# First loads on a second queue, early weight fetches and plain last stores in a fused attention, MoE and FFN kernel

## The chip, the cores and the metric
The kernel runs on one core of a Trainium2 chip. The metric is device time in microseconds (us) of one execution, lower is better. TensorE multiplies matrices (PE in the profile, PEld its weight loads); VectorE (DVE), ScalarE (ACT) and GpSimd (POOL) work on elements; SyncE (SP) issues most DMAs. A q behind an engine's name (SPq, POOLq) marks its sequencer.

## The reference
The output (2304 x 512, f32) is made in three parts:
```
scores = scale * q @ k^T            # q, k, v: (4, 8, 576, 64)
scores = where(block_i >= block_j, scores, -1e9)   # blocks of 64
x = (softmax(scores) @ v)           # tokens 2304 x 512
e = argmax(x @ w_gate)              # 8 experts, one per token
x = gate[e] * (relu(x @ w1[e]) @ w2[e])            # 512 -> 1024 -> 512
out = softplus(x @ w_in) @ w_out    # 512 -> 2048 -> 512
```

## The kernel before
**Precision.** Every f32 operand is split into a high and a low part (`h`, `l`), and each product is three matmuls: high by high, low by high, high by low. ScalarE casts the high part, VectorE subtracts it for the low one.

**Stages.** Attention runs over 16 pairs of heads (4 batches of 8 heads): k and q are transposed on TensorE (`prep_pe`, L315 to L326, K and Q in the order below; `a` for the first 512 rows, `b` for the last 64), split into `kZ` and `qZ`, and scores, exponentials, transposes and products follow. Batch 0 is loaded by `load_first` (L267 to L274) head by head, in calls f0, f1 and on; the other batches by `load_raw` (b1.0 and on). Between them the constants are set (p0 to p36, `mrow` among them) and, with `et`, the routing's tables. Then 12 slots of 256 tokens of one expert each go through the MoE: gather (g), transposes (X), first layer (A), second layer (C), output copy on ScalarE (yo, L981) and scatter by GpSimd into `yd` (sc, L986), with the weights loaded (d) and split (h1, l1, h2, l2) per slot. Slots that only other inputs need lie behind a nest of branches (`more`, L1430 to L1436). The FFN takes the tokens in groups of 4, 4, 4, 4 and 2 tiles of 128: it loads `yg` (fl for group 0, y1 to y4 after it), transposes it (fx0t to fx3t, x1.0.t and on), runs the first layer over 16 column blocks f with weights `HB[f]` (P, L1119 to L1121: 12 matmuls per group and f) and softplus (a), and stores the result to DRAM (`gd`). The second layer takes 8 chunks per group: a chunk's two blocks are loaded (N g.c.0, tile `gq`, three buffers in turn), sums of quarters are made and split (N g.c.1 to N g.c.5, `ah` and `al`), and seven products are added up instead of eight (Q, 42 matmuls a chunk in the groups of four tiles, banks X, Y, Z and M). o combines the banks into `fos`, O writes 128 rows to the output.

**Second-layer weights.** The sums of w_out's quarters are made and split during the first layer (w, s). Those of chunks 0 to 3 stay in SBUF; those of 4 to 7 are stored to `wd` in DRAM and come back by `fetch` (W4 to W7, two tiles of 896 KB each) into the pool that `second_pools` (e2, L1445) opens when the first layer's tiles are closed. A fetch waits for the last use of what lay there.

**Output rows.** The MoE's scatter puts the tokens into `yd` in a new order, and each row carries its token number in a last column; `OI` keeps it, and `done` (L1301 to L1307) scatters each finished tile to those rows by an indirect DMA of GpSimd.

**What sets the order.** One string, `SCHEDULE` (line 46), names every call; the loop at L1450 runs them one after the other, and each call appends its instructions to its engines' queues. So an engine works through its own instructions in the string's order, and one that waits holds up all behind it on that engine:
```python
        for key in SCHEDULE.split():
            if key in calls:
                calls.pop(key)()
```
Of the kernel before, what the change touches and what calls it, by code (L numbers as in the profile page):

```python
# [112 lines left out]
l17+1 lr39 h27+1 lr43 l20+1 yo1+0 lr44 l21+1 sc1+0 lr45 l22+1 lr46 A0+1 lr47 lg1 d10+2 lr49 lg2 lr50 lg3 lg4 g0+2 l23+1  # L113
d11+2 lg5 l24+1 g1+2 d12+2 lg6 l25+1 A1+1 lg7 d13+2 hh0+1 l26+1 lg8 lg9 lg10 hl0+1 lg11 d20+2 lg12 lg14 l27+1 h10+2
d21+2 l10+2 A2+1 d22+2 hh1+1 h12+2 hl1+1 d23+2 l12+2 lg15 h14+2 h16+2 l14+2 A3+1 hh2+1 l16+2 hl2+1 h11+2 lg16 h13+2
l11+2 X0+2 h15+2 l13+2 C0+1 d10+3 hh3+1 l15+2 xh0+2 d11+3 hl3+1 h17+2 C1+1 h20+2 xl0+2 d12+3 lg17 l17+2 h21+2 X1+2
l20+2 d13+3 C2+1 xh1+2 l21+2 xl1+2 d20+3 h22+2 C3+1 g0+3 l22+2 h23+2 C4+1 g1+3 l23+2 lg13 h24+2 d21+3 C5+1 l24+2 h25+2
C6+1 l25+2 h26+2 d22+3 C7+1 l26+2 yo0+1 sc0+1 A0+2 h27+2 yo1+1 l27+2 sc1+1 d23+3 A1+2 hh0+2 hl0+2 h10+3 h12+3 l10+3
A2+2 h14+3 l12+3 hh1+2 l14+3 h16+3 hl1+2 l16+3 A3+2 hh2+2 hl2+2 h11+3 h13+3 l11+3 X0+3 h15+3 l13+3 C0+2 d10+4 hh3+2
l15+3 xh0+3 d11+4 hl3+2 h17+3 C1+2 h20+3 xl0+3 d12+4 l17+3 h21+3 X1+3 l20+3 d13+4 C2+2 g0+4 xh1+3 l21+3 xl1+3 d20+4  # L120
g1+4 h22+3 C3+2 l22+3 h23+3 C4+2 l23+3 h24+3 d21+4 lg18 l24+3 C5+2 lg19 lg20 lg21 more v0+0 v1+0 v0+1 v1+1 h25+3 C6+2
# [604 lines left out]
def late_routing(nc, K, L, m, rows_of, big, wide, B):  # L726
# [763 lines left out]
```

## Time and profile before
| | |
|---|---|
| median of 3 runs | 939.73 us (937.86 to 939.75) |
| the profiled execution | 940.5 us, of which the span is 938.8 |
| mean granted clock | 0.993 |
| VectorE, ScalarE, GpSimd busy | 71%, 60%, 16% |
| DMA | 149.17 MB, mean 159 GB/s |

The span runs from the first to the last instruction; 1.7 us of the time lie around it. Busy shares are means over stages with different limits, so a change in one stage is read from the rows of that stage. The page's 40 slices of 23.5 us show TensorE at nine tenths or more but in the first, in the slices about 730 to 800 (8 and 9) and in the last (4):
```profile
PE   6999999999999999999999999999999989999994
```

### The profile page before, as it was taken

The numbers are of one execution on the slowest core, as the hardware profiler recorded it, in microseconds if no ns is written. First come the engines' busy times: TensorE is split into PE (matmuls) and PEld (weight loads), VectorE is DVE, ScalarE is ACT, GpSimd is POOL, SyncE is SP. The second block draws the span as 40 slices with busy tenths as digits, with TensorE's granted clock in tenths as the row PEclk, the third lists the DMA queues.
The fourth block names the chain that finished last, engine by engine and source line by source line (L and its number), as shares of the span: only waits on it lengthen the run. The fifth ranks groups of instructions, "written<-read, shape, count | busy, mean of one in ns | idle before, by whom it ended". The sixth has DMA issues, their size and how long they took to land.

```text
span 938.8 us, 18304 instructions
## 1 busy us (share of the span) xinstructions
PE 901.2 (96%) x6331; PEld 796.9 (85%) x6331; DVE 664.0 (71%) x1471; ACT 566.9 (60%) x1256; POOL 146.0 (16%) x183
## 2 busy tenths in 40 slices
PE   6999999999999999999999999999999989999994
PEld 4888888777999889999999887888789988999994
DVE  3766778885997888666664367686675479798874
ACT  3677676685755657555553487887788533334331
POOL 2000000010163142222221000000000003131512
PEclk9999999999999999999999999999999999999997
DMA  5984644213526398766520366556655673434421
GB/s 125 194 159 81 139 83 132 87 50 116 170 65 224 113 300 265 239 220 210 177 86 23 118 213 220 175 190 235 235 206 198 229 288 128 142 113 136 133 80 59
DMA packets 134645, 149.17 MB, mean 159 GB/s; under 512 B 70543, under 2 KB 92047, under 8 KB 134544
## 3 DMA queue, kind: packets, MB, share of 16 engines
q1 hardware_dynamic: 129264, 132.17, 46.5%
q0 software_dynamic: 5280, 15.75, 4.9%
q8 instruction: 51, 0.84, 0.4%
q14 instruction: 50, 0.41, 0.2%
HBM read 120.09 MB, written 41.96 MB: 173 GB/s over the span
## 4 chain that ended last, share of the span: by engine, by line
PE 54%; DVE 6%; DMA 3%; ACT 2%; issue 1%; SPq 0%; POOLq 0%; DVEq 0%; ACTq 0%
PE yps L975 3%; PE yps L977 3%; PE yps L976 3%; PE fh L1120 3%; PE hps L955 3%; PE fh L1119 3%; PE fh L1121 3%; PE hps L956 3%; PE hps L957 3%; DMA gq<-gd 2%; PE fX L1120 2%; PE fX L1121 2%; PE fX L1119 2%; PE fY L1120 2%; PE fY L1121 2%; PE fz L1275 2%
## 5 line engine op out<-in xcount | busy, mean ns | idle before, releaser
L1242 ACT CAST ah<-sum 128x1280 fp32r<-128x1280 f32 (+1 forms) x40 | 46.2, 1156 | 113.9 <-issue 46.0
L955 PE MATMUL hps<-xh,H1h 128*128 128x256 f32 x384 | 109.2, 284 | 1.5 <-ACT y L981 1.5
L956 PE MATMUL hps<-xl,H1h 128*128 128x256 f32 x384 | 108.7, 283 | 0.3 <-DVE xl L945 0.3
L957 PE MATMUL hps<-xh,H1l 128*128 128x256 f32 x384 | 108.6, 283 | 0.0
L383 ACT ACTIVATE P<-s,negm 128x448 f32<-128x448 f32 (+4 forms) x160 | 82.7, 528 | 25.5 <-DVE negm L378 25.5
L918 DVE TENSOR_TENSOR H2l<-R,H2h 128x512 fp32r<-128x512 f32 x96 | 67.2, 716 | 26.8 <-ACT H2h L914 26.8
L378 DVE TENSOR_REDUCE negm<-s 128x1 f32<-128x576 f32 (+4 forms) x160 | 68.2, 479 | 20.5 <-PE s L372 20.5
L975 PE MATMUL yps<-H2h,hh 128*128 128x512 f32 x192 | 77.2, 402 | 1.9 <-PEq L1432 1.9
L1303 POOL DMA_INDIRECT out_dram<-fos,OI x18 | 45.2, 2512 | 214.0 <-DVE fos L1299 177.2
L914 ACT CAST H2h<-R 128x512 fp32r<-128x512 f32 x96 | 58.0, 621 | 31.9 <-DVE H2l L918 17.8
L955 PEld LDWEIGHTS hps<-xh,H1h 128*128 128x128 f32 x384 | 73.5, 192 | 2.5 <-ACT y L981 1.7
L977 PE MATMUL yps<-H2l,hh 128*128 128x512 f32 x192 | 74.9, 390 | 0.0
L976 PE MATMUL yps<-H2h,hl 128*128 128x512 f32 x192 | 74.8, 389 | 0.0
L956 PEld LDWEIGHTS hps<-xl,H1h 128*128 128x128 f32 x384 | 73.6, 192 | 0.9 <-DVE xl L945 0.5
L918 DVE TENSOR_TENSOR H1l<-R,H1h 128x512 fp32r<-128x512 f32 x96 | 64.1, 706 | 13.4 <-ACT H1h L914 12.3
L957 PEld LDWEIGHTS hps<-xh,H1l 128*128 128x128 f32 x384 | 73.6, 192 | 0.0
L389 PE MATMUL pt<-ident,P 128*128 128x128 f32 x480 | 69.4, 282 | 2.7 <-DVE PT L394 2.0
L372 PE MATMUL s<-kZ,qZ 64*128 64x288 f32 (+4 forms) x576 | 64.2, 336 | 3.7 <-DVE qZ L343 1.5
L1246 DVE TENSOR_TENSOR al<-sum,ah 128x1280 fp32r<-128x1280 f32 (+1 forms) x40 | 54.1, 1352 | 19.1 <-ACT ah L1242 19.1
L914 ACT CAST H1h<-R 128x512 fp32r<-128x512 f32 x96 | 55.1, 619 | 18.8 <-PE hps L956 17.4
L372 PEld LDWEIGHTS s<-kZ,qZ 64*128 64x128 f32 x576 | 54.3, 198 | 12.1 <-issue 6.2
L1275 PE MATMUL fz<-Wh,al 128*128 128x256 f32 x216 | 61.8, 286 | 0.0
(287 smaller groups left out, 2608.5 us busy)
## 6 DMA issues: line engine op xcount, KB each, us to landing
R<-in_moe_w_dram SPq DMA_DIRECT2D x96, 512.0 KB
gd<-ft SPq DMA_DIRECT2D x64, 256.0 KB
gq<-gd SPq DMA_DIRECT2D x64, 256.0 KB
dbw<-in_moe_w_out_dram SPq DMA_DIRECT2D x32, 256.0 KB
dbl<-in_moe_w_in_dram SPq DMA_DIRECT2D x22, 256.0 KB
yg<-yd SPq DMA_DIRECT2D x4, 1026.0 KB
xd<-xs SPq DMA_DIRECT2D x16, 256.0 KB
wd<-ah SPq DMA_DIRECT2D x4, 896.0 KB
```

The costliest lines, as they stand in the source:

```text
L372: mm(o, lhsT=a, rhs=b, start=first, stop=last)
L383: nc.scalar.activation(t[0:n, 0:NK[c]], SC.pop((p, j, c))[0:n], AF.Exp, bias=NM.pop((p, j, c))[0:n], scale=1.0, accum_out=rs[p % 4][0:n, c ...
L389: nc.tensor.transpose(ps[:, o:o + 128], P[p, j, c][:, 128 * kc:128 * kc + 128], ident)
L914: nc.scalar.copy(HW[l, i][0], raw(l, i))
L918: TT(l_, raw(l, i), h.bitcast(F32), op=ALU.subtract)
L955: mm(a, lhsT=wh, rhs=xh, start=(k == 0), stop=False)
L956: mm(a, lhsT=wh, rhs=xl, start=False, stop=False)
L957: mm(a, lhsT=wl, rhs=xh, start=False, stop=(k == 3))
L975: mm(o, lhsT=h[:, c], rhs=wh, start=(f == 0), stop=False)
L976: mm(o, lhsT=l[:, c], rhs=wh, start=False, stop=False)
L977: mm(o, lhsT=h[:, c], rhs=wl, start=False, stop=(f == 7))
L1275: mm(o, lhsT=l, rhs=wh, start=False, stop=False)
```

## The change
- q's loads of heads 0 and 1 (four DMAs) are issued by ScalarE, first of all, with the table load `at` between them; SP's other first loads follow k directly, and v's of heads 0 and 1 come behind k and q of heads 2 and 3. `u0` adds seven bf16 matmuls of 512 columns on `mrow` before the first transposes, `u1` two more before the first scores. `et` moves behind the first pair's m01.
- The late routing places the tokens of the last two tiles (rows 2048 to 2303) in their own rows of `yd`, by five more VectorE operations; `done` writes these two tiles with two plain DMAs from SP in the place of two scatters.
- The empty case of each `tc.If` is laid out first.
- v0+5 and v1+5 (w_in's conversion) move behind yo1+3; fl moves behind sc1+10 and fx0t to fx3t behind C3+11, between C4+11 and C7+11; s5.5 to s5.7 move behind x3.3.
- `fetch` is called per tile. `e3` sets the tiles' places: the first three (W4.0, W4.1, W5.0) lie over HB[3], HB[5] and HB[7] and are fetched by GpSimd, which also issues chunk 2's load. SP fetches W5.1 behind N0.4.0, W6 behind N0.6.0, W7 behind N0.7.0.
- In the last group Q4.5.4 to Q4.5.6 move behind o4.0.2.

Of the string, pieces without the calls between them (`-` before, `+` now):
```diff
-p0 f0 f1 p1 f2 p2 f3 f4 p3 f5 p4 f6 p5 f7 f8 f9 f10 f11 f12 f13 p6
+f4 f5 at f6 f7 p0 f0 f1 p1 f2 p2 f3 p3 p4 p5 f8 f9 f10 f11 f12 f13 p6
...
-l26+4 v0+5 v1+5 A0+4 yo0+3 sc0+3 v2+5 yo1+3 v3+5
...
-a4.15.4 e2 N0.1.4 N0.2.0 W4 N0.1.5
+a4.15.4 e2 e3 W4.0 W4.1 W5.0 N0.1.4 N0.2.0 N0.1.5
```
Of the code:
```diff
-    def load_first(nm, h0, nh):
+    def load_first(nm, h0, nh, eng=nc.sync):
...
-        return [lambda o=o, i=i: nc.sync.dma_start(o, i) for o, i in l]
+        return [lambda o=o, i=i: eng.dma_start(o, i) for o, i in l]
...
+    calls["at"] = lambda: nc.scalar.preload_act_table_set("natural_log_exp_and_others")
+
+    def warm(n):
+        o = pso.tile([128, 512], F32, tag="o", name="warm")
+        for _ in range(n):
+            mm(o.rearrange("p (a b) -> p a b", a=4), lhsT=mrow, rhs=mrow.unsqueeze(1).to_broadcast([128, 4, 128]), start=True, stop=True)
+
+    calls.update(u0=lambda: warm(7), u1=lambda: warm(2))
-    first = load_first("k", 0, 2) + load_first("q", 0, 2) + load_first("v", 0, 2) + load_first("k", 2, 2) + load_first("q", 2, 2) + gates + load_first("v", 2, 2)
+    first = load_first("k", 0, 2) + load_first("q", 0, 2, nc.scalar) + load_first("k", 2, 2) + load_first("q", 2, 2) + load_first("v", 0, 2) + gates + load_first("v", 2, 2)
...
+        lambda: TT(xs, C[:, :, T - 1:T], Gx[:, :, T - 2:T - 1], op=ALU.subtract),
+        lambda: V.tensor_tensor_scan(xc, xs.rearrange("p e o -> p (e o)"), K["z"][:, 0:G], 0.0, op0=ALU.add, op1=ALU.add),
+        lambda: TT(xs, xc.unsqueeze(2), xs, op=ALU.subtract),
+        lambda: TT(Z, Z, bc(xs, 128, G, T), op=ALU.subtract),
...
+        lambda: TT(dm[:, T - 2:T], tk[:, T - 2:T, 0], tk[:, T - 2:T, 1], op=ALU.add),
...
-    def fetch(c):
-        W[c] = [P["wrest"].tile([128, 7 * QW], F32R, tag=f"W{x}{c}", name=f"W{x}{c}", bufs=1) for x in "hl"]
-        for j in range(2):
-            nc.sync.dma_start(W[c][j].bitcast(F32), wd[c, j])
+    def rest():
+        for c, j in ((5, 1), (6, 0), (6, 1), (7, 0), (7, 1), (4, 0), (4, 1), (5, 0)):
+            W.setdefault(c, [None, None])[j] = P["wrest"].tile([128, 7 * QW], F32R, name=f"W{'hl'[j]}{c}")
+
+    def fetch(c, j):
+        (nc.gpsimd if (c, j) in ((4, 0), (4, 1), (5, 0)) else nc.sync).dma_start(W[c][j].bitcast(F32), wd[c, j])
...
-                nc.sync.dma_start(t[:, j, 0:w], gd[16 * g + c + 8 * j, :, 0:w])
+                (nc.gpsimd if n == 2 else nc.sync).dma_start(t[:, j, 0:w], gd[16 * g + c + 8 * j, :, 0:w])
...
+        if i >= NT // 128 - 2:
+
+            nc.sync.dma_start(out[128 * i:128 * i + 128], st["out", g, u][:, 2 * j:2 * j + 2].rearrange("p a b -> p (a b)"))
+            return
...
-                    nest.enter_context(tc.If(n > s - EARLY))
+                    nest.enter_context(tc.If(n > s - EARLY, preferred_fallthrough_block=False))
```
ScalarE's queue at the start, before and now (`psT` is the bank of the transposes; a number behind a tile's name is only its buffer):
```order
L1371 ACT_TABLE_LOAD
L338 ACTIVATE kZ<-psT 128x512
L338 ACTIVATE qZ<-psT 128x512
L338 ACTIVATE qZ<-psT_259 128x64
L338 ACTIVATE kZ<-psT_259 128x64
```
```order
L274 DMA qraw<-in_q_dram 128x4x64 x2
L486 ACT_TABLE_LOAD
L274 DMA qraw<-in_q_dram 64x2x64 x2
L338 ACTIVATE kZ<-psT 128x512
L338 ACTIVATE qZ<-psT 128x512
```
Four DMAs of q stand ahead of ScalarE's first casts, two on either side of the table load.

SP's queue behind the last stores of the first layer (L1137, now L1153), before and now (L1213, now L1231, is a fetch of a weight tile; L1223, now L1241, a chunk's load):
```order
L1137 DMA gd<-ft 128x256 x16
L1223 DMA gq_12916<-gd 128x512 x2
L1213 DMA Wh_12919<-wd 128x1792
L1213 DMA Wl_12920<-wd 128x1792
L1223 DMA gq_12936<-gd 128x512 x2
L1213 DMA Wh_12939<-wd 128x1792
L1213 DMA Wl_12940<-wd 128x1792
L1223 DMA gq_12951<-gd 128x512 x2
L1213 DMA Wh_12954<-wd 128x1792
L1213 DMA Wl_12955<-wd 128x1792
L1223 DMA gq_13016<-gd 128x512 x2
```
```order
L1153 DMA gd<-ft 128x256 x16
L1241 DMA gq_12959<-gd 128x512 x2
L1231 DMA Wl_12927<-wd 128x1792
L1241 DMA gq_12971<-gd 128x512 x2
L1241 DMA gq_13032<-gd 128x512 x2
L1231 DMA Wh_12928<-wd 128x1792
L1231 DMA Wl_12929<-wd 128x1792
L1241 DMA gq_13092<-gd 128x512 x2
L1231 DMA Wh_12930<-wd 128x1792
L1231 DMA Wl_12931<-wd 128x1792
L1241 DMA gq_13152<-gd 128x512 x2
```
Chunk 2's load and three fetches left the queue; the loads for chunks 4, 5, 6 and 7 stand behind no fetch, one, one and three.

GpSimd's queue from there to the end, now (L1123 copies `OI`, L1325 is the scatter of the output, of which 18 stood here before):
```order
L1123 COPY OI<-yg 128x2
L1231 DMA Wh_12932<-wd 128x1792
L1231 DMA Wl_12933<-wd 128x1792
L1231 DMA Wh_12934<-wd 128x1792
L1241 DMA gq_12943<-gd 128x512 x2
L1325 DMA out_dram<-fos,OI 2304x512 x16
```
Three fetches and chunk 2's load came ahead of the scatters, and the last two scatters are gone.

## Rows read from the trace of the kernel before

**Rows 1.** The page, part 1: busy time, share of the span, instructions.
```profile
PE 901.2 (96%) x6331; PEld 796.9 (85%) x6331; DVE 664.0 (71%) x1471; ACT 566.9 (60%) x1256; POOL 146.0 (16%) x183
```

**Rows 2.** Windows: length, busy us (instructions) by engine, granted clock, DMA share, GB/s.
```profile
0.00:30.00 30.00, 20.63 (x111) 17.24 (x111) 12.89 (x38) 13.51 (x40) 5.95 (x49) 1.00 0.59 132
720.00:730.00 10.00, 10.00 (x86) 10.00 (x86) 3.47 (x9) 8.46 (x23) 0.00 (x0) 1.00 0.35 117
735.00:795.00 60.00, 54.64 (x428) 53.01 (x427) 47.16 (x92) 23.14 (x40) 5.31 (x2) 0.97 0.63 231
745.00:765.00 20.00, 17.05 (x137) 16.24 (x135) 13.41 (x25) 7.54 (x13) 0.00 (x0) 1.00 1.00 401
800.00:860.00 60.00, 60.00 (x502) 60.00 (x502) 49.63 (x96) 23.48 (x38) 15.08 (x6) 1.00 0.42 132
```

**Rows 3.** Waits of TensorE: us in total, times, longest us.
```profile
PE fY L1275 <- DVE al L1246: 3.7, 6, 1.1
```

**Rows 4.** Chain that ended last, 735 to 786: start us, us, what.
```profile
740.73 9.51 DMA gq<-gd
...
754.53 7.18 DMA gq<-gd
...
765.99 2.91 DMA gq<-gd
```

**Rows 5.** Timeline, 0 to 31: start, us, engine line, what [idle before <-releaser].
```profile
0.83 1.28 ACT L1371 ACT_TABLE_LOAD   x1 [0.83 <-PEq L1474]
...
1.09 0.27 DVE L299 MEMSET mrow<- 1x64 bf16 x2
...
3.31 2.44 SPq L274 DMA_DIRECT2D qraw<-in_q_dram  x4
...
5.28 0.60 ACT L338 ACTIVATE kZ<-psT 128x512 fp32r<-128x512 f32 x1 [3.17 <-PE psT L326]
...
6.87 1.09 PE L326 MATMUL psT<-ident,qraw 128*128 128x128 f32 x4 [1.62 <-DMA qraw<-in_q_dram]
...
20.72 3.56 SPq L274 DMA_DIRECT2D qraw<-in_q_dram  x6
...
28.38 0.93 PE L389 MATMUL pt<-ident,P 128*128 128x128 f32 x7
...
29.26 0.27 PE L326 MATMUL psT<-ident,qraw 128*128 128x128 f32 x1
```

**Rows 6.** Line 1432 (tc.If): duration ns min/median/max; who waited, us, times.
```profile
L1432 PEldq COMPARE_BRANCH  x1: 3472/3472/3472, 305.4 to 305.4; - x1
...
  PE yps L975: 1.9, 1
```

**Rows 7.** Timeline of TensorE, 341 to 344 and 664 to 672.
```profile
342.54 0.39 PE L955 MATMUL hps<-xh,H1h 128*128 128x256 f32 x1 [1.47 <-ACT y L981]
...
668.87 0.50 PE L1120 MATMUL fY<-fxl,HBh 128*128 128x512 f32 x1 [0.77 <-DVE fxl L1105]
```

**Rows 8.** Timeline of GpSimd and TensorE, 498 to 526.
```profile
505.77 0.98 POOL L986 DMA_INDIRECT yd<-y,k_si  x1 [2.82 <-DMA yd<-y,k_si]
...
524.57 0.39 PE L1119 MATMUL fh<-fxh,HBh 128*128 128x512 f32 x1
```

**Rows 9.** Line 986 (scatters to yd), its transfers.
```profile
DMA to landing us min/median/max: 3.3/4.7/6.9
```

**Rows 10.** Chain that ended last, 915 to 939.
```profile
926.79 0.43 DVE fos L1299
...
927.98 2.77 DMA out_dram<-fos,OI
```

**Rows 11.** Line 1485 (the program's end): duration ns min/median/max, first and last start.
```profile
L1485 POOLq DRAIN  x3: 40/112/6660, 931.3 to 938.5; - x3
```

**Rows 12.** Line 1303 (scatters of the output), its instructions and transfers.
```profile
L1303 POOL DMA_INDIRECT out_dram<-fos,OI x18: 971/1226/10210, 786.7 to 931.5; - x18
...
DMA to landing us min/median/max: 2.7/3.0/12.1
```

More of the change, by code (lines that the diff above doesn't have):

```diff
@@ L117 @@
[L117 to L121, printed above, removed]
@@ new lines @@
+d12+3 lg22 l17+2 h21+2 X1+2 l20+2 d13+3 C2+1 xh1+2 l21+2 xl1+2 d20+3 h22+2 C3+1 g0+3 l22+2 h23+2 C4+1 g1+3 l23+2 lg18
+h24+2 d21+3 C5+1 l24+2 h25+2 C6+1 l25+2 h26+2 d22+3 C7+1 l26+2 yo0+1 sc0+1 A0+2 h27+2 yo1+1 l27+2 sc1+1 d23+3 A1+2
+hh0+2 hl0+2 h10+3 h12+3 l10+3 A2+2 h14+3 l12+3 hh1+2 l14+3 h16+3 hl1+2 l16+3 A3+2 hh2+2 hl2+2 h11+3 h13+3 l11+3 X0+3
+h15+3 l13+3 C0+2 d10+4 hh3+2 l15+3 xh0+3 d11+4 hl3+2 h17+3 C1+2 h20+3 xl0+3 d12+4 l17+3 h21+3 X1+3 l20+3 d13+4 C2+2
+g0+4 xh1+3 l21+3 xl1+3 d20+4 g1+4 h22+3 C3+2 l22+3 h23+3 C4+2 l23+3 h24+3 d21+4 lg23 l24+3 C5+2 lg24 lg25 lg26 more
@@ new lines @@
+l13+11 C0+10 hh3+10 l15+11 xh0+11 hl3+10 h17+11 C1+10 h20+11 xl0+11 l17+11 h21+11 X1+11 l20+11 C2+10 xh1+11 l21+11
+xl1+11 h22+11 C3+10 l22+11 h23+11 C4+10 l23+11 h24+11 C5+10 l24+11 h25+11 C6+10 l25+11 h26+11 C7+10 l26+11 yo0+10
+sc0+10 A0+11 h27+11 yo1+10 l27+11 sc1+10 fl A1+11 hh0+11 hl0+11 A2+11 hh1+11 hl1+11 hh2+11 A3+11 hl2+11 hh3+11 C0+11
+hl3+11 C1+11 C2+11 C3+11 fx0t fx0h C4+11 fx0l fx1t fx1h C5+11 fx1l fx2t fx2h C6+11 fx2l fx3t fx3h fx3l C7+11 yo0+11
+sc0+11 P0.1.0 yo1+11 P0.1.1 sc1+11 ep c11.-1 P0.0.0 P0.0.1 P0.0.2 P0.0.3 P0.1.2 a0.0.0 P0.1.3 c9.0 c9.1 a0.0.1 P0.2.0
@@ new lines @@
+c9.2 a0.0.2 y1 P0.2.1 c9.3 c10.0 P0.2.2 a0.0.3 a0.1.0 c10.1 P0.2.3 a0.0.4 c9.4 c10.2 a0.1.1 P0.3.0 c9.5 a0.2.0 P0.3.1
+c10.3 a0.1.2 P0.3.2 a0.2.1 a0.1.3 c10.4 P0.3.3 a0.1.4 a0.2.2 c10.5 P0.4.0 a0.3.0 a0.2.3 P0.4.1 c11.0 c11.1 a0.2.4
+a0.3.1 P0.4.2 c11.2 a0.3.2 P0.4.3 c11.3 c12.-1 P0.5.0 a0.3.3 a0.4.0 P0.5.1 c11.4 a0.3.4 a0.4.1 c11.5 P0.5.2 a0.4.2
+P0.5.3 a0.4.3 P0.6.0 a0.5.0 a0.4.4 P0.6.1 c12.0 c12.1 P0.6.2 a0.5.1 c12.2 a0.5.2 P0.6.3 c12.3 c13.-1 P0.7.0 a0.5.3
+a0.6.0 P0.7.1 c12.4 a0.5.4 a0.6.1 c12.5 P0.7.2 a0.6.2 P0.7.3 c13.0 c13.1 P0.8.0 P0.8.1 a0.6.3 a0.7.0 P0.8.2 c13.2
@@ new lines @@
+a0.7.1 a0.6.4 P0.8.3 c13.3 c14.-1 a0.7.2 P0.9.0 a0.8.0 a0.7.3 P0.9.1 c13.4 a0.7.4 a0.8.1 c13.5 P0.9.2 a0.8.2 P0.9.3
+a0.8.3 P0.10.0 a0.9.0 a0.8.4 N0.0.0 P0.10.1 a0.9.1 c14.0 c14.1 P0.10.2 a0.9.2 P0.10.3 c14.2 a0.9.3 P0.11.0 a0.10.0
+c14.3 P0.11.1 a0.10.1 c14.4 P0.11.2 a0.9.4 c15.-1 N0.1.0 a0.10.2 c14.5 P0.11.3 a0.10.3 P0.12.0 a0.11.0 P0.12.1 a0.11.1
+P0.12.2 a0.11.2 P0.12.3 a0.11.3 x1.0.t a0.12.0 P0.13.0 a0.10.4 a0.11.4 x1.0.h P0.13.1 a0.12.1 x1.0.l c15.0 P0.13.2
+c15.1 a0.12.2 P0.13.3 c15.2 a0.12.3 x1.1.t a0.13.0 P0.14.0 c15.3 w0.0 x1.1.h a0.12.4 P0.14.1 a0.13.1 x1.1.l c15.4
@@ new lines @@
+P0.14.2 a0.13.2 c15.5 P0.14.3 a0.13.3 x1.2.t a0.14.0 P0.15.0 a0.13.4 w0.1 w0.2 P0.15.1 x1.2.h P0.15.2 w0.3 a0.14.1
+P0.15.3 x1.2.l a0.14.2 w0.4 w0.5 P1.0.0 a0.15.0 a0.14.3 x1.3.t a0.15.1 P1.0.1 a0.14.4 x1.3.h P1.0.2 a0.15.2 x1.3.l y2
+w0.6 P1.0.3 a0.15.3 w0.7 P1.1.0 a0.15.4 P1.1.1 a1.0.0 w0.8 P1.1.2 a1.0.1 w0.9 w1.0 P1.1.3 a1.0.2 s0.0 P1.2.0 a1.1.0
+a1.0.3 P1.2.1 a1.1.1 s0.1 a1.0.4 s0.2 P1.2.2 a1.1.2 s0.3 s0.4 P1.2.3 a1.1.3 s0.5 P1.3.0 a1.1.4 P1.3.1 s0.6 P1.3.2
+a1.2.0 w1.1 P1.3.3 a1.2.1 P1.4.0 w1.2 a1.3.0 P1.4.1 w1.3 a1.2.2 P1.4.2 a1.3.1 w1.4 w1.5 a1.3.2 P1.4.3 a1.2.3 w1.6
@@ new lines @@
+P3.7.0 a3.6.0 P3.7.1 a3.5.2 a3.6.1 P3.7.2 a3.5.3 s6.8 w7.1 w7.2 P3.7.3 a3.5.4 a3.6.2 w7.3 P3.8.0 a3.7.0 a3.6.3 P3.8.1
+a3.7.1 w7.4 w7.5 P3.8.2 a3.7.2 a3.6.4 N0.1.1 P3.8.3 a3.7.3 P3.9.0 N0.1.2 a3.8.0 a3.7.4 P3.9.1 a3.8.1 N0.1.3 P3.9.2
+a3.8.2 P3.9.3 a3.8.3 P3.10.0 a3.8.4 a3.9.0 P3.10.1 a3.9.1 P3.10.2 a3.9.2 P3.10.3 a3.9.3 w7.6 w7.7 P3.11.0 a3.9.4
+a3.10.0 P3.11.1 w7.8 a3.10.1 P3.11.2 w7.9 a3.10.2 P3.11.3 s7.0 a3.10.3 P3.12.0 a3.11.0 s7.1 a3.10.4 P3.12.1 s7.2
+a3.11.1 s7.3 P3.12.2 s7.4 a3.11.2 s7.5 P3.12.3 a3.11.3 x4.0.t a3.11.4 P3.13.0 s7.6 P3.13.1 x4.0.h s7.7 a3.12.0 P3.13.2
@@ L248 @@
+Q4.7.2 Q4.7.3 o4.0.1 o4.0.2 Q4.5.4 Q4.5.5 Q4.6.4 Q4.6.5 Q4.7.4 Q4.7.5 o4.0.3 Q4.5.6 Q4.6.6 Q4.7.6 o4.0.4 O4.0.0 O4.0.1
 """
@@ L1342, in ffn @@
         if c >= NWR:
-            add(f"W{c}", fetch, c)
+            for j in range(2):
+                add(f"W{c}.{j}", fetch, c, j)
+    add("e3", rest)
     return calls
```

315 lines of the change are left out of this document (145 added, 170 removed).

## The prediction
> **What bounds the kernel now.** First the page's busy times: TensorE is busy 901.2 of the 938.8 us span [rows 1], so about 37.6 us of idle time is all that a change of order can win, besides what TensorE loses to a lower pace. Then windows: in a quiet stretch of the second FFN layer TensorE takes 502 matmuls in 60 us without a gap, 0.1195 us each, but only 428 in the 60 us where that layer begins [rows 2]. The missing 74 are worth 74 x 0.1195 = 8.8 us. Then what TensorE waits for: there, mostly the residuals `al` of VectorE [rows 3]; and the chain of waits says why VectorE is late: the chunk loads `gq` before them take 9.51 and 7.18 us, an undisturbed one 2.91 [rows 4]. The rest of the idle time is at the two ends and in a few single holes.
>
> **q's loads and the warm matmuls.** SP issues each first load in about 0.61 us (2.44 us for q's four), and TensorE waits 1.62 us for q's landing before its second transposes [rows 5]. On ScalarE's queue q's first two loads leave at once and the other two behind the table load of 1.28 us; all take 0.83 + 4 x 0.61 + 1.28, so ScalarE is free at about 4.5, ahead of its first work at 5.28 [rows 5]: the move costs it nothing. Everything that SP issues after k comes 2.44 us earlier; v's first loads, now behind q's second pair, leave at about 8.2 instead of 5.8 and are wanted only after the first exponentials. The early tables leave VectorE's path to the first scores.
>
> How much of it lasts? Four transposes take 1.09 us at 6.87, and seven take 0.93 us at 28.38 [rows 5]: the array runs at half pace up to there, that of 1.2 GHz and not 2.4, though the clock column shows 1.00 for this stretch [rows 2]. A load lands some 2.9 us after its issue [rows 4]. q's last two parts, issued by 4.5, land at 7.4: the first pair gains under 1 us. The gain comes later, and q's loads for pair 2 limit it: issued from 20.72 to 24.28, they land by 27.2, and feed the transpose at 29.26 [rows 5]. 2.44 us earlier is 24.7: no more than 29.26 - 24.7 = 4.6 us can be won. If the array stays at half pace, the gain is only the earlier issue, 2.4 us. If the seven and two warm matmuls, put where the array is idle, bring the full pace from about 5 us on, it reaches the bound. They cost little: 0.12 us per 256 columns at full pace [rows 2] is 0.48 us per 512 at half pace, 3.4 us for seven; begun when `mrow` is set, at 1.4 [rows 5], they end at 4.8, and k's transposes behind them still end before q's last parts land. I take **-4**, with -1.5 (half pace, and a part given back to VectorE) and -4.6 as ends.
> The Trainium skill (TensorE: Matmul & The Clock Gate, Part 4: PE-mode transpose) says that transposes do not count as array work for the clock, so that before the first scores only other matmuls could raise it. By that rule the warm ones are what is missing and the term is -4.6; if they change nothing, it is -2.4.
>
> **The branch.** TensorE's compare-and-branch over the extra slots takes 3.47 us, and TensorE stands 1.9 us for it [rows 6]. The path taken now falls into the empty case and jumps over the bodies from there. The way is as long, so I take 0; ends -1.9 (the hole closes) and +0.5 (the second jump costs a part of the first).
>
> **Single holes.** The conversions v0+5 and v1+5 stood ahead of the output copy `y` on ScalarE, in wait for a load; TensorE waited 1.47 us for `y` [rows 7]. They move behind it: **-1.5** (ends 0 and -1.5). The sums s5.6 stood ahead of the last `fxl` of group 3 on VectorE; TensorE waited 0.77 [rows 7]: **-0.8** (ends 0 and -1.5, since s5.5 on ScalarE moves too). Five more small VectorE operations in the late routing lie where TensorE has no gap: 0, or +1 if a routing matmul comes late.
>
> **The first group's tokens.** `fl` now waits for slot 10's scatters. The second starts at 505.77 [rows 8] and one lands in 3.3 to 6.9 us [rows 9], so `yg`'s load (1 MB) starts at 509 to 512.7. It takes the 2.91 us of a half-megabyte chunk load and 1.3 for the other half at 401 GB/s: it is there at 513.3 to 516.9. Its transposes are moved too: behind fx0t stand four C of six matmuls of 0.23 us and four transposes of 0.44 us, 7.3 us, before the first FFN matmul at 524.57 [rows 8], so fx0t comes at 517.3. The cost is 0, with 0.4 to 4 us to spare; past that each late microsecond costs one.
>
> **The fetched weights.** Eight tiles of 896 KB come back from DRAM, 7.3 MB with chunk loads between them, and in 745 to 765 the DMA engines are full at 401 GB/s [rows 2]. Three of them (W4.0, W4.1, W5.0) now lie over layer-1 weights of f = 3, 5 and 7. Twelve, ten and eight f's of twelve matmuls of 0.1195 us stand behind the last use of these before layer 1 ends at 735.4, so they are free at about 718, 721 and 724, where the DMA engines are 0.35 busy [rows 2]. GpSimd has nothing else there; it issues them and chunk 2's load behind them, so its waits hold up nobody. SP's fetches are 2.75 MB less, 6.9 us of transfer at 401 GB/s, and chunk 4's load goes ahead of them all: 9.51 becomes about 2.9. Chunk 6's keeps one tile ahead of it (2.3 us: 7.18 becomes about 5.2). Chunk 7's and the next have two ahead, 7.5 us, but with three chunk buffers they are issued two chunks of 42 x 0.1195 = 5.0 us ahead. I take **-7** of the 8.8, since some is VectorE's own backlog at the group's end; ends -2 and -8.8.
> The Trainium skill (DMA: Bandwidth & Descriptors, Issuing engines are not separate DMA queues) speaks against this part: DMAs from any queue run on the same 16 engines, and a second issuer saves only the issue time. The full 401 GB/s agree that the engines are shared. By that rule the term would be 0; I hold against it that the tiles also come earlier.
>
> **The tail.** The last `fos` starts at 926.79; the first scatter lands after 2.77 us [rows 10], the second waits for it, and POOL's drain, from 931.3 on, takes 6.66 us [rows 11], to 937.96. 0.84 us later the span ends. Now two plain stores leave at 927.3 and 927.6, land some 2.9 us after an issue of 0.3, at 930.8 [rows 4, 10], and SP's closing checks (0.6) and the same 0.84 make 932.3. POOL's drain starts behind the last scatter of group 3, at 922 to 925; at its whole 6.66 us it is over by 932. **-6**, ends -4 (slower stores, of which no row tells) and -6.9. The reordered last nine matmuls: 0.
>
> **Sum.** -4 - 1.5 - 0.8 - 7 - 6 = -19.3 against the profiled 940.5 us: 921.2. The median of the runs is 0.8 us below it, so I forecast **921 us**, with 916 to 926 for this case by itself.
>
> **Rivals.**
> Shared engines: the early fetches crowd the last stores of layer 1, or SP's five tiles still fill the chunk loads' time, and the 8.8 us stay. For it: 401 GB/s; against it: 0.35 before 735 [rows 2]. 921 + 7 = 928. This is the page's rule named above.
> Half pace: the array is not raised, the first four transposes still take 1.09 us, and what VectorE needs eats the earlier issue. 921 + 4 = 925.
> All at its end: branch -1.9, start -4.6, fetches -8.8, holes -3, tail -6.9 make -25.2: 915.
> Slower, through GpSimd's queue: a scatter of 256 KB landed in 3.0 us as a rule and 12.1 at worst [rows 12], and the next waited for it. If the three fetches, each larger, go one behind the other at 12.1 us from 725, chunk 2's load behind them lands at 725 + 36.3 + 2.9 = 764, 22 us after its old time of some 742. The fetches' 7 us are lost and 22 come on top: 921 + 7 + 22 = 950. It makes the kernel slower than before from (742 + 12.3 - 2.9 - 725)/3 = 8.8 us per fetch on, where 12.3 are the other terms. Against it: the same tiles moved at 401 GB/s, 2.3 us each, from SP.
>
> **Chances.** The forecast 0.62, shared engines 0.15, half pace 0.10, all at its end 0.07, slower 0.06. The range of 915 to 928 takes in the first four by their values; with their own spread some 0.14 fall out, and the slower case with them. Faster by over 0.2% (1.9 us, about what a measurement of this kernel can tell from no change) is 0.94, the first four; within it 0.01; slower 0.05.
>
> **What would show it.** In the changed profile: q's first transposes before 6.5 us, four transposes in 0.6 us well before 20; no wait on `y` near 340; a DMA share well over 0.35 before the second layer, the chain's `gq` pieces under 6 us, some 490 matmuls in the 60 us after layer 1; no scatter behind the last `fos`, and some 5.5 us from its start to the span's end. The prediction is wrong if TensorE still lacks 60 matmuls there, if a POOL transfer stands in the chain, or if the drain still ends last.

## The result and the profile after

The median went from 939.04 us (937.86 to 939.75) to **928.3 us** (928.19 to 930.94): a ratio of 0.9894, interval 0.9872 to 0.9915. The kernel is faster by 10.7 us, forecast were 18; the time lies 0.3 us above the range. The profiled execution took 928.19 us, 926.5 of them span, against 940.5 and 938.8.

The page's busy times, to be held against [rows 1], and its slices of TensorE:
```profile
PE 904.3 (98%) x6340; PEld 798.2 (86%) x6340; DVE 665.0 (72%) x1476; ACT 568.0 (61%) x1256; POOL 156.0 (17%) x186
PE   8999999999999899999999999999999999999997
```
The span is 12.3 us shorter, but TensorE is busy 3.1 us longer. The nine warm matmuls (3.17 and 1.06 us, below) alone are more than that. The dent of the slices about 730 to 800 is closed, and a new 8 stands in the slice from 301 to 324. Where the time went is found by setting the start of the same TensorE instruction in the two traces side by side, from the start to the end:

| place (us in the trace of after) | forecast | measured |
|---|---|---|
| start, up to pair 2's last transposes (25.6) | -4 | -3.7 |
| 24 matmuls of `o` at 177 | none | +1.7 |
| branch at 305: the hole, and half pace behind it | 0 | +1.9, +1.6 |
| `y` at 340 | -1.5 | -1.7 |
| `fxl` at 668 | -0.8 | -1.0 |
| entry to the second layer, 734 to 789 | -7 | -3.4 |
| all the rest, up to the last `fos` (921.76) | 0 | -0.4 |
| from the last `fos` to the span's end | -6 | -7.3 |
| sum | -19.3 | -12.3 |

The start, in TensorE's part of the timeline of after (columns as in [rows 5]):
```profile
1.42 3.17 PE L491 MATMUL warm<-mrow 128*128 128x512 bf16 x7 [1.42 <-DVE mrow L299]
...
6.21 1.06 PE L326 MATMUL psT<-ident,qraw 128*128 128x128 f32 x4
...
7.49 1.06 PE L491 MATMUL warm<-mrow 128*128 128x512 bf16 x2
...
10.88 0.60 PE L326 MATMUL psT<-ident,qraw 128*128 128x128 f32 x4
...
22.69 1.06 PE L326 MATMUL psT<-ident,kraw 128*128 128x128 f32 x4
...
25.57 0.27 PE L326 MATMUL psT<-ident,qraw 128*128 128x128 f32 x1
```
q's first transposes start at 6.21, the wait for `qraw` is gone, and four transposes take 0.60 us at 10.88: the signs that were named. But at 22.69 four take 1.06 us again, so the full pace did not last; still the last transpose of the stretch starts at 25.57 and no longer at 29.26 [rows 5]. SP's own timeline shows how much earlier its loads leave:
```profile
0.82 6.04 SPq L274 DMA_DIRECT2D kraw<-in_k_dram  x8
...
19.35 3.56 SPq L274 DMA_DIRECT2D qraw<-in_q_dram  x6
```
q's loads for pair 2 leave at 19.35 instead of 20.72 [rows 5], which is 1.4 us, where 2.44 were forecast: SP's first eight loads of k take 6.04 us and not 8 x 0.61 = 4.9, since SP stands for 1.2 us ahead of the seventh.

Windows of after (columns as in [rows 2]): the branch, the fetches' stretch, and the second layer's first 60 us with two pieces of it.
```profile
308.00:314.00 6.00, 4.99 (x17) 4.14 (x18) 4.91 (x13) 2.43 (x5) 0.10 (x1) 0.72 0.32 92
716.00:732.00 16.00, 16.00 (x137) 16.00 (x136) 4.25 (x10) 10.64 (x32) 2.73 (x5) 1.00 0.96 334
735.00:740.00 5.00, 2.84 (x20) 2.59 (x21) 2.04 (x5) 4.81 (x12) 0.00 (x0) 1.00 0.36 123
740.00:744.00 4.00, 4.00 (x23) 4.00 (x22) 4.00 (x9) 0.78 (x2) 0.00 (x0) 0.57 0.33 86
735.00:795.00 60.00, 57.20 (x457) 56.58 (x458) 50.85 (x100) 26.53 (x47) 8.82 (x2) 0.97 0.55 189
```
The 60 us behind 735 hold 457 matmuls: 29 more than before [rows 2], where 490 were forecast. In 735 to 740 TensorE is idle for 2.2 us, and in the 4 us after that the granted clock is 0.57 and 23 matmuls pass where 33 do at full pace. By the starts of the same matmuls 4.1 us are lost against before from 734 to 744 (2.6 by the hole, 1.5 by the pace), and 7.5 are won from there to 789. The waits of TensorE in 735 to 795 and of ScalarE in 715 to 740, in after, name what came late:
```profile
PE fX L1292 <- DVE ft L1151: 1.7, 1, 1.7
PE fX L1292 <- DVE fw L1311: 0.6, 1, 0.6
PE fY L1292 <- DVE ft L1151: 0.6, 1, 0.6
```
```profile
ACT ft L1145 <- DMA gd<-ft: 5.0, 3, 2.8
```
ScalarE had no room for a finished block of layer 1: its `ft` buffers were still being stored to `gd`. The chain of after from 708 to 800 shows these stores, and GpSimd's timeline what ran beside them:
```profile
718.41 4.96 DMA gd<-ft
...
724.65 6.56 DMA gd<-ft
...
738.48 0.43 DVE ft L1151
738.96 0.39 PE fX L1292
```
```profile
717.69 0.58 POOL L1231 DMA_DIRECT2D Wh<-wd  x1 [47.55 <-DVE ft L1151]
720.43 0.56 POOL L1231 DMA_DIRECT2D Wl<-wd  x1 [2.16 <-PE fY L1137]
723.30 0.53 POOL L1231 DMA_DIRECT2D Wh<-wd  x1 [2.31 <-PE fh L1137]
723.82 1.07 POOL L1241 DMA_DIRECT2D gq<-gd  x2
```
The three fetches start within 0.7 us of the forecast 718, 721 and 724. With them the DMA engines are 0.96 busy in 716 to 732, and two stores of the last blocks take 4.96 and 6.56 us. ScalarE waits 5.0 us in all, finishes layer 1 late, and TensorE stands for the last `ft`. But no `gq` load stands any more in the chain over this stretch ([rows 4] had three).

The branch: its instructions in TensorE's queue (columns as in [rows 6]), and TensorE's timeline around it.
```profile
L1455 PEldq COMPARE_BRANCH  x2: 95/1786/3477, 303.5 to 305.5; - x2
...
L1455 PEldq EVENT_SEMAPHORE  x1: 51/51/51, 305.3 to 305.3; - x1
```
```profile
304.89 0.39 PE L993 MATMUL yps<-H2l,hh 128*128 128x512 f32 x1
309.01 0.50 PE L991 MATMUL yps<-H2h,hh 128*128 128x512 f32 x1 [3.73 <-issue]
...
310.97 0.63 PE L992 MATMUL yps<-H2h,hl 128*128 128x512 f32 x1
```
There are two jumps now. The short one (95 ns) starts at 303.5. The long one (3477 ns) stands behind a semaphore at 305.3, which comes just when the last matmul ends (304.89 + 0.39 = 305.28), and lasts from 305.5 to 308.98. Before, the long one started at 305.4 while queued matmuls still ran, up to 307.16, which hid 1.8 us of its 3.47; now all of it lies bare, and TensorE stands 3.73 us where it stood 1.85. Behind the hole the matmuls take 0.63 us instead of 0.39, and the clock granted in 308 to 314 is 0.72, which was 1.00 before.

The end of the chain of after, and the drain (columns as in [rows 11]):
```profile
921.76 0.42 DVE fos L1317
```
```profile
L1508 POOLq DRAIN  x3: 44/113/7785, 915.7 to 926.2; - x3
L1508 SPq DRAIN  x3: 7/7/13, 925.6 to 925.9; - x3
```
No scatter stands behind the last `fos`. GpSimd's long drain starts right after its last scatter, and, begun at 915.7, is over by 923.5. SP's own, behind the two stores, starts at 925.6. From the last `fos` to the span's end it is 4.7 us, where it was 12.0 [rows 10, 11].

### The profile page after: what moved, and what is told of

Same layout as the page of the kernel before. It is cut to its first block, busy times and chain, and to the rows that moved or that the text cites. A ratio compares the mean times of both kernels' runs of the same rounds, so it can differ in the third digit from the quotient of the medians.

```text
span 926.5 us, 18335 instructions
## 1 busy us (share of the span) xinstructions
PE 904.3 (98%) x6340; PEld 798.2 (86%) x6340; DVE 665.0 (72%) x1476; ACT 568.0 (61%) x1256; POOL 156.0 (17%) x186
## 4 chain that ended last, share of the span: by engine, by line
PE 63%; ACT 1%; DMA 1%; issue 1%; DVE 1%; DVEq 0%; ACTq 0%
PE hps L971 4%; PE hps L972 4%; PE hps L973 4%; PE yps L991 4%; PE yps L993 4%; PE yps L992 4%; PE fz L1294 3%; PE fz L1292 3%; PE fz L1293 3%; PE fh L1136 3%; PE fh L1135 3%; PE fh L1137 3%; PE fX L1136 2%; PE fX L1292 2%; PE fX L1137 2%; PE fX L1135 2%
## 5 line engine op out<-in xcount | busy, mean ns | idle before, releaser
L934 DVE TENSOR_TENSOR H2l<-R,H2h 128x512 fp32r<-128x512 f32 x96 | 66.5, 709 | 26.9 <-ACT H2h L930 26.9
L1325 POOL DMA_INDIRECT out_dram<-fos,OI x16 | 49.5, 3092 | 143.4 <-DVE fos L1317 107.7
L1294 PE MATMUL fz<-Wl,ah 128*128 128x256 f32 x216 | 61.8, 286 | 0.0
```

Source lines behind the costliest of these rows:

```text
L934: TT(l_, raw(l, i), h.bitcast(F32), op=ALU.subtract)
L1294: mm(o, lhsT=h, rhs=wl, start=False, stop=last)
```

## The experiments

Three explanations of the shortfall stood against each other: new waits that the change itself makes (the second jump, the full `ft` buffers); a term that is not there at all, since the DMA engines are shared whoever issues; and gains that are real but lost again at the next wait. Each kernel is the changed one with the edit shown, but for z1. The kernel before took 940.6 us beside the x runs, 938.36 beside the y runs and 938.63 beside the z runs.

**x1_noflag**: the empty case of the branch is laid out last again.
```diff
-tc.If(n > s - EARLY, preferred_fallthrough_block=False)
+tc.If(n > s - EARLY)
```


> The changed kernel without the flag that lays the empty case of each branch first; all else stays. Theory (the flag adds a second jump that TensorE's queue stands for): the hole before the first matmul behind the branch shrinks from 3.7 us to the 1.9 us of before, the array does not fall to half pace behind it, and the time is 928.3 - 3.7 = 924.6 us. Rival (the longer hole comes from where the code lies or from a late engine): the hole stays above 3 us and the time at 928.3 us.


Measured: 927.47 us (926.32 to 929.03), ratio 0.986 (0.9833 to 0.9886). One jump stands there again, and the hole is 1.8 us:
```profile
L1455 PEldq COMPARE_BRANCH  x1: 3452/3452/3452, 302.2 to 302.2; - x1
```
```profile
305.83:310.33 4.50, 4.50 (x13) 3.59 (x14) 2.87 (x9) 2.46 (x6) 0.00 (x0) 0.62 0.24 66
```
The hole shrinks by 1.9 us, as the edit was to give, but in this profile half pace follows the shorter hole as well. The median falls by 0.8 us where 3.7 were expected, and the intervals of the two ratios overlap: the size of the hole is shown here, its worth in the time is not.

**x2_half**: the last group's blocks of 128 x 256 share an `ft` buffer two by two, so that its five buffers hold ten.
```diff
-st["t", g, f] = P["fact"].tile([128, 512], F32, tag="ft", name="ft", bufs=5)[:, 0:w]
+if w == 512 or f % 2 == 0:
+    st["t"] = P["fact"].tile([128, 512], F32, tag="ft", name="ft", bufs=5)
+st["t", g, f] = st["t"][:, 0:w] if w == 512 or f % 2 == 0 else st["t"][:, w:2 * w]
```


> The changed kernel, but the last group's blocks of 128x256 share a buffer of 128x512 two by two, so that ten and not five of them may wait for their store. Theory (GpSimd's early fetches fill the DMA engines, the last stores of the first layer take 5 to 6.6 us, ScalarE waits for buffers and TensorE stands for its results at the layer's end): ScalarE's 5.0 us of waits for gd go, TensorE's hole of some 2.3 us at 737 to 739 and the half pace behind it (1.4 us) go, and the time is 928.3 - 3.5 = 924.8 us. Rival (the hole has another cause, or the stores only shift it to the chunk loads behind them): 928.3 us, or up to 1 us less.


Measured: 926.67 us (925.03 to 929.27), ratio 0.9849 (0.9822 to 0.9876). The DMA engines are as full as without the edit (0.96 in 716 to 732), but ScalarE's wait for them is gone and TensorE stands 4.1 us better than in after at 744. It loses 3.2 us again at 780, and 1.5 at half pace behind that. TensorE's waits, a window behind the later hole, and the chunk loads in the chain of x2:
```profile
PE fX L1294 <- DVE fw L1313: 3.3, 2, 2.7
```
```profile
782.00:786.00 4.00, 4.00 (x24) 4.00 (x23) 4.00 (x11) 0.00 (x0) 1.03 (x1) 0.57 0.19 70
```
```profile
745.40 4.73 DMA gq<-gd
...
758.10 9.56 DMA gq<-gd
```
So the stall for `ft` was the full buffers, and it hid the next limit: a chunk load behind two fetched tiles takes 9.56 us, VectorE is late from there on, and TensorE waits for the group's combination `fw` at 780. So the gain at 744 is real and is lost again at the next wait. By the medians 1.6 us are left, which is not clear of the noise.

**x3_wsp**: all fetches and chunk 2's load go to SP, at their places in the string.
```diff
-(nc.gpsimd if (c, j) in ((4, 0), (4, 1), (5, 0)) else nc.sync).dma_start(W[c][j].bitcast(F32), wd[c, j])
+nc.sync.dma_start(W[c][j].bitcast(F32), wd[c, j])
...
-(nc.gpsimd if n == 2 else nc.sync).dma_start(t[:, j, 0:w], gd[16 * g + c + 8 * j, :, 0:w])
+nc.sync.dma_start(t[:, j, 0:w], gd[16 * g + c + 8 * j, :, 0:w])
```


> The changed kernel with the three early fetches and chunk 2's load back on SP, at their places in the order, so behind the last stores of the first layer; the tiles lie where the change puts them. Theory (the early time of the three fetches is the gain): the missing matmuls in the 60 us after layer 1 go from 45 back to some 74, no wait for gd on ScalarE, and the time is 928.3 + 29 x 0.12 = 931.8 us. Rival (the early fetches bring nothing and only crowd the stores): without the crowding the time falls by 3 to 925 us.


Measured: 933.12 us (931.22 to 934.9), ratio 0.9917 (0.9889 to 0.9945). A window and the longest waits of TensorE and VectorE in 735 to 795:
```profile
735.00:795.00 60.00, 50.20 (x385) 49.30 (x384) 43.90 (x87) 20.22 (x34) 3.43 (x2) 0.91 0.61 220
```
```profile
PE fY L1292 <- ACT ah L1260: 5.5, 1, 5.5
```
```profile
DVE sum L1247 <- DMA gq<-gd: 16.1, 4, 8.1
```
Without the early time only 385 matmuls pass, 72 fewer than in after. That is more than the early time alone: chunk 2's load now stands behind three tiles on SP's queue, where before had none ahead of it, and 385 are also 43 fewer than before. The DMA engines are 0.35 busy in 716 to 732 here and 0.96 in after, so the gain is that 2.75 MB move before 735. The Trainium skill (DMA: Bandwidth & Descriptors, Issuing engines are not separate DMA queues) says that DMAs of all issuers run on the same engines; the 0.96 of after agrees, but sharing does not make the term 0.

**x4_nowarm**: no warm matmuls.
```diff
-p22 u0 Kta.0 b1.9
+p22 Kta.0 b1.9
...
-Klb.0 u1 S0.0
+Klb.0 S0.0
```


> The changed kernel without the warm matmuls u0 and u1. Theory A (they raise the array's pace early, and that is worth what is left above the earlier issue): four transposes at 10 to 12 us take 1.09 us again, pair 2's transposes come at 27 instead of 25.5 us, and the time rises by 1.4 to 929.7 us. Theory B (the start is paced by loads and the other engines): unchanged at 25.5, time 928.3 us. The stretch of half pace at 177 to 181, 1.7 us long, tells besides whether it hangs on the start: if it goes, the time is 1.7 us lower in either case.


Measured: 928.54 us (927.33 to 931.29), ratio 0.9877 (0.9844 to 0.991). The transposes in TensorE's timeline of x4:
```profile
11.23 1.06 PE L326 MATMUL psT<-ident,qraw 128*128 128x128 f32 x4
...
25.74 0.27 PE L326 MATMUL psT<-ident,qraw 128*128 128x128 f32 x1
```
At 11.23 the transposes take 1.06 us where after had 0.60. In the profiles of all runs, q's four transposes of pair 1 take 0.60 to 0.63 us in eight of the nine with warm matmuls (1.06 in x2) and 1.06 to 1.08 in the three without (before, x4, z1): the warm matmuls mostly raise the pace there. The Trainium skill (TensorE: Matmul & The Clock Gate, Part 4: PE-mode transpose) says that transposes do not count as busy time for the clock in the way that other matmuls do; the rows agree with that, but x2 shows that the warm matmuls alone don't settle the pace. Pair 2's last transpose starts at 25.74 against 25.57, and the median is the same: no worth of this pace in the time is shown.

**y1_gpall**: x1 and x2 together, and all eight tiles fetched by GpSimd, so that SP's queue has chunk loads alone.
```diff
-(nc.gpsimd if (c, j) in ((4, 0), (4, 1), (5, 0)) else nc.sync).dma_start(W[c][j].bitcast(F32), wd[c, j])
+nc.gpsimd.dma_start(W[c][j].bitcast(F32), wd[c, j])
```


> The changed kernel without the branch flag, with the shared half buffers of the last group, and with all eight weight tiles fetched by GpSimd, so that SP's queue holds only chunk loads after layer 1. Known from the runs before: the flag costs 2.05 us; with the half buffers alone 4.0 us are won by 744 us and given back at 780, where TensorE stands 2.7 us for VectorE's `fw`, and 1.5 us at half pace. Theory (VectorE is late at 780 because chunk loads stand behind weight tiles on SP's queue, 4.7 and 9.56 us long in the chain): the chunk loads fall under 5 us, the hole at 780 goes below 1 us, and the time is 926.7 - 2 - 3 = 921.5 us. Rival (VectorE's own work per chunk is the bound there): the hole stays over 2 us, 924.7 us.


Measured: **922.08 us** (920.05 to 926.18), ratio 0.9815 (0.979 to 0.984). The window behind layer 1, the chunk load that is left in the chain, and TensorE's waits in 300 to 360:
```profile
735.00:795.00 60.00, 59.80 (x496) 59.39 (x496) 53.38 (x104) 27.40 (x47) 14.33 (x7) 1.00 0.56 194
```
```profile
746.58 3.13 DMA gq<-gd
```
```profile
PE yps L991 <- PEq L1457: 2.0, 1, 2.0
PE hps L971 <- DVE hl L981: 1.8, 1, 1.8
```
496 matmuls: the 490 that the prediction wanted. The entry to the second layer now gains (496 - 428) x 0.1195 = 8.1 us, and y1, which has neither the full buffers nor SP's tiles, shows no wait of TensorE over 0.2 us in it. A hole of 1.8 us is new at 345, where conversions of w_in that wait for their load stand ahead of `hl` on VectorE.

**y2_spread**: x1 and x2, and SP's tiles one behind each chunk's load, never two.
```diff
-N0.5.0 Q0.0.3
+N0.5.0 W6.0 Q0.0.3
...
-N0.6.0 W6.0 W6.1 Q0.1.3
+N0.6.0 W6.1 Q0.1.3
...
-N0.7.0 W7.0 W7.1 Q0.2.3
+N0.7.0 W7.0 Q0.2.3
...
-N1.0.0 Q0.3.3
+N1.0.0 W7.1 Q0.3.3
```


> As the run with all tiles on GpSimd, but the five later tiles stay on SP, one behind each chunk load (W5.1, W6.0, W6.1, W7.0, W7.1 behind the loads for chunks 4 to 8), instead of two at a time. Theory (two tiles ahead of a chunk load make it 9.56 us): no chunk load in the chain over 6 us, the hole at 780 under 1.5 us, 922 us. Rival (VectorE's own work): 924.7 us.


Measured: **921.87 us** (919.71 to 925.84), ratio 0.9819 (0.9793 to 0.9846). The window and the chunk loads in the chain:
```profile
735.00:795.00 60.00, 59.42 (x495) 59.22 (x494) 54.17 (x107) 24.79 (x40) 13.77 (x2) 1.00 0.59 193
```
```profile
745.94 4.61 DMA gq<-gd
758.66 6.08 DMA gq<-gd
```
The same from the other side: SP may carry the tiles, as long as no chunk load waits for two of them. 9.56 became 6.08 us. These two are the fastest versions, 1.8% below the kernel before and apart from after by their intervals.

**y3_scatter**: the last two tiles go out by scatters again.
```diff
-        if i >= NT // 128 - 2:
-            nc.sync.dma_start(out[128 * i:128 * i + 128], st["out", g, u][:, 2 * j:2 * j + 2].rearrange("p a b -> p (a b)"))
-            return
```


> The changed kernel with the last two tiles written by GpSimd's two indirect scatters again (to the same rows, which the index column holds). Theory (the second scatter waits for the first and POOL's drain begins only behind it): the span ends some 11 us after the last fos starts instead of 4.7, and the time is 928.3 + 6.2 = 934.5 us. Rival (the end is set by what every program does there): 928.3 us.


Measured: 935.72 us (932.48 to 938.97), ratio 0.9969 (0.9953 to 0.9985), 7.4 us above after. From `fos` at 921.46 to the span's end at 933.8 it is 12.3 us, of which the drain alone, behind the last scatter, takes 7.08:
```profile
L1504 POOLq DRAIN  x3: 44/112/7080, 925.9 to 933.6; - x3
```
The tail is worth what the table gives (-7.3): most of the 10.7 us that the whole change won.

**y4_qsp**: q's first loads are issued by SP again, behind k's; v's stay behind.
```diff
-f4 f5 at f6 f7 p0 f0 f1 p1 f2 p2 f3 p3 p4 p5
+at p0 f0 f1 p1 f2 p2 f3 f4 p3 f5 p4 f6 p5 f7
...
-load_first("q", 0, 2, nc.scalar)
+load_first("q", 0, 2)
```


> The changed kernel with q's first four loads back on SP behind k's, and everything else as changed (v's loads still behind q's second pair, the tables later, the warm matmuls there). Theory (ScalarE's queue gives the start's 3.8 us, by 2.4 us of earlier issue at the least): pair 2's last transposes come at 28 to 29.3 instead of 25.6 and the time is 931 to 932 us. Rival (the start's gain is v's place in the order and the tables', which also bring pair 1's and pair 2's loads forward): they stay at 25.6 to 26.5, 928.3 to 929 us.


Measured: 930.08 us (927.54 to 933.1), ratio 0.991 (0.9881 to 0.9939). Pair 2's last transposes start at 26.9, 1.3 us later than in after and 2.4 earlier than before. This does not yet give the second queue's worth: the eight profiles with the same start as after (after, x1, x2, x3, y1, y2, y3, z2) have these transposes anywhere from 24.6 to 26.7, and the median is not clear of after's. What does hold in every profile is the issue: SP's loads of q for pair 2 leave at 20.7 without ScalarE's queue (before, y4, z1) and at 19.0 to 19.4 with it.

**z1_order**: the kernel before with one edit: v's first loads behind q's second pair, and the routing's tables later.
```diff
-load_first("v", 0, 2) + load_first("k", 2, 2) + load_first("q", 2, 2)
+load_first("k", 2, 2) + load_first("q", 2, 2) + load_first("v", 0, 2)
...
-Qla.0 et p36 Qlb.0
+Qla.0 p36 Qlb.0
...
-m01.0 Kla.1
+m01.0 et Kla.1
```


> The kernel before, with only two parts of the change: v's first loads behind q's second pair, and the early tables behind the first pair's m01; q stays on SP, no warm matmuls. Theory (these two give most of the start's 3.8 us, ScalarE's queue about 1 and the warm matmuls nothing): pair 2's last transposes at 26 to 27.5 instead of 29.26, and 2 to 3 us less than before: 936 to 937 us beside 939. Rival (without ScalarE's queue the order gains nothing): 29.3 and no difference.


Measured: 937.06 us (935.5 to 939.08), ratio 0.9982 (0.997 to 0.9994) to the kernel before. In its timeline:
```profile
26.75 0.30 PE L327 MATMUL psT<-ident,qraw 128*128 128x128 f32 x1 [1.08 <-DMA qraw<-in_q_dram]
```
29.26 became 26.75, on one queue and without a warm matmul, though q's loads for pair 2 leave at 20.73, as before. By the medians the order of the loads and tables gives 1.6 us, clear of the noise.

**z2_flag**: y1 with the empty case first, as in after.
```diff
-tc.If(n > s - EARLY)
+tc.If(n > s - EARLY, preferred_fallthrough_block=False)
```


> The run with all tiles on GpSimd and shared half buffers, with the branch flag put back. Theory (the flag makes two far jumps of one): the hole behind the branch is 3.5 to 3.9 us instead of 2.0, often with half pace behind it, and the time is 922 + 1.9 to 3.5 = 924 to 925.5 us. Rival (what the flag costs is taken back at the next wait, the conversions near 345 us that wait for loads): the hole is there, the time is 922 to 923 us.


Measured: 923.01 us (921.76 to 925.75), ratio 0.9831 (0.9817 to 0.9845). TensorE's waits in 300 to 360 and the stretch behind the branch:
```profile
PE yps L991 <- issue: 4.0, 1, 4.0
PE hps L971 <- DVE hl L981: 1.0, 1, 1.0
```
```profile
310.00:315.00 5.00, 4.47 (x11) 3.51 (x12) 4.66 (x12) 1.32 (x3) 0.00 (x0) 0.50 0.34 99
```
The hole is 2 us longer and half pace stands behind it, yet the median is only 0.9 us above y1's, and the intervals overlap: the wait for `hl` at 345, 1.8 us in y1, is 1.0, and half pace does not follow it. What TensorE loses at the branch it waits less at 345, where a load is late either way; that reading fits the rows, and no further run separates it. So the second jump costs some 2 us of hole (3.5 to 4.0 us in the seven profiles with it, 1.8 to 2.1 in the five without); by the times it is 0.8 and 0.9 us in x1 and z2, and neither is clear of the noise.

## Why the prediction was too low

**The direction and four terms held.** The start gave -3.7 for -4, `y` -1.7 for -1.5, `fxl` -1.0 for -0.8, and the first group's tokens cost nothing. The tail gave -7.3, beyond its end of -6.9: GpSimd's drain is over 2.1 us before SP's begins (923.5 and 925.6; the forecast had it end at 932), so it holds up nothing, and y3 brings 7.4 us back.

**One profile does not reach far.** Each kernel has one profile, and equal code does not cost the same in each. The entry to the second layer has the same code in after, x1, x4, y3 and y4; set against before it gives -3.4, -1.0, -0.7, -2.8 and -4.3. In z1, whose entry is that of before, it gives -2.1. So a row of the table that moves by less than some 2 us proves little by itself, and what follows leans on several profiles with the same edit where there are some. The rows of `y` and `fxl` do hold: -1.7 and -1.0 stand in all ten profiles with these edits.

**The start came near its number in part by luck.** The text let the warm matmuls bring the full pace, and gave -2.4 if they change nothing. They mostly raise the pace at 10 to 12 us, but it falls back (1.06 us for four transposes at 22.69), and x4 without them is no slower. Nor did the loads leave 2.44 us earlier: it was 1.4. The order of v's loads and the tables, to which the step gave no price of its own, brings 2.5 us in z1's profile and 1.6 by its medians. In the eight profiles with this start the gain is 2.6 to 4.7 us, so a measured -3.7 is no proof of -4, and how it divides between order and queue stays open.

**The step that failed most: "The fetched weights".** It was -3.4 for -7. The early fetches were placed "where the DMA engines are 0.35 busy", and their own effect on what kept the engines 0.35 busy was not priced: the stores of layer 1, behind which ScalarE has only five buffers. That is the first half of the rival of the shared engines ("the early fetches crowd the last stores of layer 1"). It cost 4.1 us up to 744; behind that 7.5 us were won. All five profiles with early fetches and five buffers (after, x1, x4, y3, y4) lose 2.8 to 4.4 us there, and none of the four with early fetches and shared buffers (x2, y1, y2, z2) loses any. The second miss is in "Chunk 7's and the next have two ahead, 7.5 us": with two tiles ahead a load took 9.56 us in x2, which the three buffers do not cover. TensorE waits 3.3 us for `fw` there in x2, 2.4 and 3.2 in x1 and x4, and 0.6 in after. x2 takes away the first limit and shows the second; y1, y2 and z2 take away both and have 496, 495 and 500 matmuls in the 60 us, 8.1, 8.0 and 8.6 us, inside the stated ends of -2 and -8.8. So the term was a fair estimate of the plan and not of this code.

That the time lies at that rival's 928 is chance: the fetches lost 3.6 of its 7 us, and the rest was lost at the branch and behind it and in `o`.

**"The branch" had the wrong structure.** "The way is as long, so I take 0", with +0.5 as the worst. The length was right (3477 against 3472 ns). But the place of the long jump moved behind the end of the queued matmuls, so what had hidden 1.8 us of it was gone: +1.9 of hole, shown by x1 and z2. Before it counts as free, a jump needs the question that every other edit was asked: what hides it, and is that still there?

**The pace behind a hole had no price.** At the branch and at 740 the array worked for some 3.5 us at about half its pace: +1.6 and +1.5. The third place, the 24 matmuls at 177 (5.04 us for 3.35), is no effect of the change that any run ties to an edit: behind the same wait of 0.97 to 0.98 us, six of the twelve profiles have 5.04 and six 3.35, and x1 and y3, the same as after up to there, are among the latter. It is +1.7 in this one profile.

The shortfall of the profile, 7.0 us, is then: fetches 3.6, branch 1.9 and 1.6, `o` 1.7, start 0.3, less 1.3 of the tail and 0.8 of small things. By the medians it is 7.3 against 921; the text's own sum, 921.2 less 0.8, makes 920.4.

## What to carry to other kernels

Moving a transfer to a quiet time fills that time: look up which stores run there, how many buffers stand behind them, and what waits when each takes 5 us or more. A load that paces an engine should not stand behind two large transfers on its queue (9.56 us here, 6.08 behind one); spread them, or give them another queue. A plain store in the place of a scatter at the program's end can be worth more than all the rest (7.3 of 10.7 us here): in before, after and y3 the long drain of GpSimd's queue, 6.7 to 7.8 us, starts only with its last scatter.

## What was not expected of the hardware

- A compare-and-branch of TensorE's queue takes 3.26 to 3.76 us in the twelve profiles when it jumps far, and 95 ns in the seven that have a near one. Hidden is only what lies beside work already queued (1.8 us in before).
- After holes, TensorE often runs at the lower of its two levels for 3 to 5 us. With the empty case first (after, x2, x3, x4, y3, y4, z2) the hole at the branch was 3.5 to 4.0 us, and half pace followed in six of seven profiles; with one jump (before, x1, y1, y2, z1) it was 1.8 to 2.1 us, and half pace followed in one of five, x1 (0.62 granted). What decides between equal holes stays open: no run here tells it.
- The granted clock can miss this: in x4 the column shows 1.00 for the first 30 us, while four transposes take 1.06 us. The duration of equal instructions is the safer row.
- SP's first eight loads of k take 5.7 to 6.0 us to issue in the nine profiles in which ScalarE issues q's beside them; where SP issues alone (before, y4, z1), two sets of four take 2.43 to 2.44 us each. What holds SP ahead of the seventh load is not shown.
- Why the wait at 345 comes and goes between y1 (1.8 us), y2 (1.6) and z2 (1.0) and after (none) stays open.
